# Later second layers, gates rounded by GpSimd and another order of slices, while a fused attention and MLP kernel decodes its weights

## The chip, the cores and the metric

The kernel runs on one core of a Trainium2 chip. The metric is device time in microseconds (us) of one execution; the kernel before takes 677.55 us, the median of three runs (677.43 to 677.74). "Span" is the time from the first to the last instruction of the one profiled execution.

Engines are called as the profile calls them: PE (TensorE, matmuls), PEld (its weight loads), DVE (VectorE), ACT (ScalarE), POOL (GpSimd) and SP (SyncE, which issues the transfers here). Each works through its own list of instructions in order.

## The reference

Attention for 4 sequences of 768 rows and 8 heads of 64, with 8 global and 96 local keys a row and a distance bias, and then an MLP on its output, 3072 rows of 512:

```python
scores = scale * q @ k.T - slope * dist          # masked to local and global keys
x = softmax(scores) @ v                          # 3072 x 512
h = x @ w_in                                     # 512 -> 2048
g = h * clip(h + 3.0, 0.0, 6.0) / 6.0            # the gate
out = g @ w_out                                  # 2048 -> 512, fp32
```

q, k and v are float32. The weights arrive as float64 numbers, of which the core receives the two 32-bit words.

## The kernel before, in words

**Blocks and slices.** The 3072 rows are eight blocks of 384. The hidden width of 2048 is cut into 16 slices of 128. For a slice f of a block b the MLP does a *first layer*, called Fb.f here (`first`, 12 matmuls of L179 into one PSUM bank hp, of which there are two), and a *second layer*, Sb.f (`second`, 9 matmuls of L211, added into three accumulator banks). Every fp32 product is made of three: a high part times both parts of the other, and its low part times the high one. So between the two layers a slice's gate has four steps: ACT adds 3 and clips at 0 (g, L190), DVE clips at 6 and multiplies by h read from PSUM (g, L191), the high part is rounded off (gh: L199 on ACT, or L197 on POOL), and DVE takes the remainder (gl, L204). The tile g has one buffer, so L190 of the next slice waits until gl of this one has read it. gh and gl have three buffers each. In a second layer, of each three matmuls two read gh and one reads gl.

**Decoding.** The weights come in 16 chunks of 1 MB, even ones for first layers and odd ones for second layers: chunk 2k serves the first layers of slices 2k and 2k+1 and chunk 2k+1 their second layers. `decode` turns a chunk's float64 words into a float32 number and splits it in two parts: L384 on ACT and L388 on POOL read the two words, DVE clamps (L417) and shifts (L418), ACT writes signs (L395), DVE adds both words (L427), ACT rounds the high part (L431) and DVE takes the remainder (L424). POOL's result of L388, the tile we, has a single buffer: L388 of the next chunk waits until L427 of this chunk has read it. The raw chunks have two buffers, wz has two.

**Stages.** First, attention of blocks 0 and 1, four pairs of heads each, with the first chunks decoded beside it. Then, as a generator (`halves`), slices of block 0 with some early slices of block 1 between them, while the other chunks are decoded. Then the other slices of block 1, beside which attention of block 2 runs, and from there each block's MLP beside the attention of the next one.

**What sets the order.** The table of `order` says in which sequence slices come. `halves` issues Fb.f, then the second layer of the slice before, and after each piece `work` lets decoding steps out while an estimate of DVE's time is behind one of PE's. On PE, POOL and SP the written order is pinned (`in_order`); on DVE and ACT a scheduler sets it when the program is built. So a POOL instruction that waits holds up all POOL instructions written behind it, and the same goes for a DVE or ACT instruction in the order that the scheduler has given.

Of the kernel before, what the change touches and what calls it, by code (L numbers as in the profile page):

```python
# [26 lines left out]
NF = DF // P  # L27
# [21 lines left out]
LEAD = 6  # L49
WAKE = 9  # L50
BESIDE = 12
LEAST_AHEAD = 4
WORDS = 2
DOWN = 2.0 ** -95

# [7 lines left out]
class Kernel:  # L63
# [377 lines left out]
    def decode_step(self):  # L441
        self.given[1] += next(self.decoding_steps)
        self.decoded += 1
        if self.decoded == 3 * (NF + 1):
            self.decoded_all()

    def decoded_to(self, i):

        while self.decoded < 3 * (i + 1) + (2 if i < NF - 1 else 3):
            self.decode_step()  # L450

    def halves(self, steps, pool=False):


        for block, f, x, acc in steps:
            self.decoded_to(f // 2 * 2)
            g = self.gate(self.first(f, x), block == len(self.blocks) - 1 and f == NF - 1)
            gh = self.high(g, pool) if pool else None
            self.work(2.1, 0.47)
            yield  # L460
            if not pool:
                gh = self.high(g, pool)
            gl = self.rest(g, gh)
            self.work(0, 0.47)
            if self.last is not None:
                self.finish()
                yield
            self.last = (block, f, acc, gh, gl)

    def end(self, steps):  # L470

# [14 lines left out]
        self.second(*late[2], (2,))  # L486

    def finish(self):
        block, f, acc, gh, gl = self.last
        self.decoded_to(f // 2 * 2 + 1)  # L490
        self.second(f, acc, gh, gl)
        if f == NF - 1 and block < len(self.blocks) - 1:
            b, tb = self.blocks[block]
            self.store(b * S + tb * TB, acc)
        self.ended = block, f
        self.work(2.1, 0)
        self.last = None

    def banded(self, flag):

        self.banded_setup()
        start = len(self.nc.cur_bb.bb.instructions)
        self.common(2, 2)
        self.ps_s = self.pool("ps_s", 1, PSUM)
        self.ps_t = self.pool("ps_t", 1, PSUM)
        self.ps_x = self.pool("ps_x", 1, PSUM)
        self.turn, self.more, self.mid, self.score_banks = {}, True, False, 1
        self.wake()
        self.raw, self.z, self.e, self.given, self.decoded = {}, {}, {}, [0.0, 0.0], 0
        self.last, self.op, self.ended = None, None, None  # L510
        self.weights()
        with ExitStack() as early, ExitStack() as words:
            x0 = self.x_tiles(self.pool("x0", 1, ctx=early, side="right"))
            xs = [x0, self.x_tiles(), self.x_tiles()]
            self.decoding(words, WORDS, (2, 1), side="right")
            self.decoding_steps = self.decode()

            def decoded_all():
                words.close()
                self.op = self.pool("op", 2, ctx=early, side="right")  # L520

            self.decoded_all = decoded_all
            self.fetch(0)
            self.given[1] = LEAD
            self.allowed = 3 * NF // 2 + 2
            acc = []
            with ExitStack() as ctx:
                self.room += self.rooms(self.pool("more", 1, ctx=ctx), MORE - ROOMS, ROOMS)
                self.load(2, False)
                self.fetch(1)  # L530
                for n in range(ROOMS):
                    self.load(n, True)
                self.plain_distances(ctx)
                self.attending(ctx, 0, 9, 5)
                pairs = [Pair(self, n, xs[n // NPAIR], True) for n in range(EARLY)]
                acc1 = []
                todo = self.halves(self.order(xs, acc, acc1))
                for n in range(-2, EARLY + 1):
                    if n + 2 < NPAIR:
                        self.distances(n + 2)  # L540
                    if n + 2 == EARLY:
                        self.more = False
                        acc.extend(self.acc_tiles())
                    if n + 2 < EARLY:
                        weigh = []
                        for t in range(NT):
                            weigh.append(pairs[n + 2].scores(t))
                            if n == 0 and t < NT - 1:
                                self.spin(2)
                        if n < 0:  # L550
                            self.spin(5)
                        self.load_next(n + 2, False)
                        self.work(1.440, 0)
                    for t in range(NT):
                        if n + 2 < EARLY:
                            weigh[t]()
                            self.work(0, 0.64)
                            if t == NT - 1 and n == -2:
                                self.load(2, True)
                        if 0 <= n < EARLY:  # L560
                            pairs[n].turn(t)
                            if n == 0 and t < NT - 1:
                                self.spin(3)
                            self.work(0.396, 0)
                        if n + 1 in (0, 1):
                            pairs[n + 1].sum_up(t)
                            pairs[n + 1].normalize(t)
                        if t == 0:
                            if 2 <= n + 1 < EARLY:
                                pairs[n + 1].sum_up()  # L570
                            if not self.more:
                                next(todo)
                        if t == 1:
                            if n > 0:
                                pairs[n - 1].values()
                                self.work(1.350, 0.47)
                            if 2 <= n + 1 < EARLY:
                                for u in range(NT):
                                    pairs[n + 1].normalize(u)
                        if t == 2 and not self.more:  # L580
                            next(todo)
            self.weights()
            self.allowed = 3 * (NF + 1)
            acc1 += [pool.tile([P, BANK], F32, name=name) for pool, name in ((self.ps_s, "sp"), (self.ps_t, "tp"), (self.ps_x, "xp"))]
            while self.ended != (0, NF - 1):
                next(todo)
        self.attending(self.ctx, 2, 4, 2, side="right")
        self.bp = self.pool("bp", 2, side="right")
        self.there = self.pool("there", 2, bass.MemoryType.DRAM)
        self.op = self.pool("op", 2, side="right")  # L590
        self.mid = True
        units = self.beside(xs[2])
        for k, _ in enumerate(todo):
            for unit in units[k] if k < len(units) else ():
                unit()
        self.mid = False
        self.score_banks = 2
        x, ahead = xs[2], None
        for i in range(2, len(self.blocks)):
            units, x_next = [], None  # L600
            if i + 1 < len(self.blocks):
                x_next = self.x_tiles()
                units, ahead = self.attention(i + 1, x_next, ahead)
                if i == 2:
                    units = [[]] + units
            else:
                units = [[]] * 4 + [[lambda: self.doubt(flag)]]
            acc = self.acc_tiles()
            steps = [(i, f, x, acc) for f in range(NF)]
            for k, _ in enumerate(self.halves(steps if x_next else steps[:-3], True)):  # L610
                for unit in units[k] if k < len(units) else ():
                    unit()
            if not x_next:
                self.end(steps[-3:])
            x = x_next
        self.in_order(start)
        return acc

    def order(self, xs, acc, acc1):


        steps, done = [], 0
        for f in range(NF):
            steps.append((0, f, xs[0], acc))
            while done * (NF - LEAST_AHEAD) < (f + 1 - LEAST_AHEAD) * (NF - BESIDE):
                steps.append((1, done, xs[1], acc1))
                done += 1
        return steps + [(1, f, xs[1], acc1) for f in range(done, NF)]
# [406 lines left out]
```

## Time and profile before

| | before |
|---|---|
| median of three runs | 677.55 us (677.43 to 677.74) |
| profiled execution, own time | 679.32 us |
| its span | 677.5 us |
| PE busy | 655.5 us (97%) |
| DVE busy | 406.7 us (60%) |
| ACT busy | 294.3 us (43%) |
| POOL busy | 212.3 us (31%) |
| granted PE clock, mean over the span | 0.989 |

The profiled execution is 1.77 us above the median of the runs. PE is busy nearly everywhere, so time is lost or won only where PE stands still: in attention of the first two blocks and while the weights are decoded, that is, up to about 125 us. Where a row of a view carries a line L..., it is the line of the source; "idle" in brackets is the time for which the engine had waited before the instruction, and what ended it.

### The profile page before, as it was taken

Reading aid. Unit: us, or ns where it says so; the run is one execution under the profiler, and the core shown is the slowest. Engines: PE = TensorE matmul, PEld = TensorE weight load, DVE = VectorE, ACT = ScalarE, POOL = GpSimd, SP = SyncE. Lnnn points to the kernel's source line nnn. Section 1 sums busy time; section 2 is a strip of 40 time slices with the busy share of each in tenths; the row PEclk is TensorE's granted clock in tenths of the full one; section 3 lists DMA queues with packets and bytes.
Section 4 is the critical chain, followed back from the end, with each engine's and each line's share of the span. In section 5 each row is a group of like instructions: output and inputs, shape, how many; then the busy total and the mean of one; then the engine's idle time right before and its main releaser. Section 6 shows DMA issues by size and latency. Waiting matters only on the chain.

```text
span 677.5 us, 11187 instructions
## 1 busy us (share of the span) xinstructions
PE 655.5 (97%) x3923; PEld 582.1 (86%) x3923; DVE 406.7 (60%) x1068; ACT 294.3 (43%) x714; POOL 212.3 (31%) x373
## 2 busy tenths in 40 slices
PE   9878898999998999999999999999999999999997
PEld 7667787898787999999998999899998999999995
DVE  6778899524564776557662677547763677422222
ACT  6988899434553444143332444143331433221111
POOL 5744232001221333325340444404541344302110
PEclk9969899999999999999999999999999999999999
DMA  8645655003575357634554257634455155500001
GB/s 321 185 162 180 247 218 186 1 1 97 153 210 156 98 156 194 171 105 125 153 157 126 91 148 194 172 112 117 125 164 156 62 154 150 139 33 18 1 1 51
DMA packets 67169, 89.56 MB, mean 132 GB/s; under 512 B 10656, under 2 KB 53920, under 8 KB 65056
## 3 DMA queue, kind: packets, MB, share of 16 engines
q1 hardware_dynamic: 66816, 88.49, 43.8%
q8 instruction: 33, 0.54, 0.3%
q14 instruction: 32, 0.26, 0.1%
q10 hardware_dynamic: 288, 0.26, 0.1%
HBM read 65.14 MB, written 23.59 MB: 131 GB/s over the span
## 4 chain that ended last, share of the span: by engine, by line
PE 75%; DVE 9%; DMA 5%; issue 4%; ACT 4%; POOL 2%; SPq 0%; POOLq 0%; DVEq 0%; ACTq 0%
PE hp L179 33%; PE acc L211 31%; PE xp L953 3%; PE sp L866 2%; ACT n L881 2%; DMA load<-pairs 2%; DVE wz L427 2%; PE tp L953 2%; PE tp L866 2%; POOL n L901 1%; DVE n L877 1%; DVE wz L417 1%; DMA wst<-w 1%; DVE g L191 1%; DVE gl L204 1%
## 5 line engine op out<-in xcount | busy, mean ns | idle before, releaser
L190 ACT ACTIVATE g<-hp,small 128x384 f32<-128x384 f32 x127 | 73.6, 580 | 246.0 <-PE hp L179 228.5
L179 PE MATMUL hp<-xh,w1h 128*128 128x384 f32 x512 | 174.6, 341 | 0.0
L179 PE MATMUL hp<-xh,w1l 128*128 128x384 f32 x512 | 172.9, 338 | 0.0
L179 PE MATMUL hp<-xl,w1h 128*128 128x384 f32 x512 | 172.5, 337 | 0.0
L197 POOL TENSOR_SCALAR gh<-g 128x384 fp32r<-128x384 f32 x96 | 51.8, 540 | 296.6 <-DVE g L191 257.5
L211 PE MATMUL acc<-w2h,gl 128*128 128x512 f32 x336 | 133.7, 398 | 5.4 <-DVE gl L204 5.4
L901 POOL TENSOR_SCALAR n<-n,sums 128x232 f32<-128x232 f32 (+1 forms) x186 | 99.0, 548 | 108.6 <-ACT n L881 61.1
L211 PE MATMUL acc<-w2h,gh 128*128 128x512 f32 x336 | 132.4, 394 | 0.4 <-ACT gh L199 0.4
L211 PE MATMUL acc<-w2l,gh 128*128 128x512 f32 x336 | 132.3, 394 | 0.0
L191 DVE SCALAR_TENSOR_TENSOR g<-g,hp 128x384 f32<-128x384 f32 x128 | 69.8, 545 | 89.8 <-ACT g L190 89.4
L881 ACT ACTIVATE n<-n,least 128x232 f32<-128x232 f32 (+1 forms) x192 | 89.2, 466 | 50.5 <-DVE least L877 49.8
L204 DVE TENSOR_TENSOR gl<-g,gh 128x384 fp32r<-128x384 f32 x128 | 78.4, 613 | 52.5 <-POOL gh L197 44.9
L179 PEld LDWEIGHTS hp<-xh,w1h 128*128 128x128 f32 x512 | 96.7, 189 | 6.0 <-issue 2.2
L179 PEld LDWEIGHTS hp<-xl,w1h 128*128 128x128 f32 x512 | 96.7, 189 | 3.7
L179 PEld LDWEIGHTS hp<-xh,w1l 128*128 128x128 f32 x512 | 96.5, 188 | 0.0
L211 PEld LDWEIGHTS acc<-w2h,gl 128*128 128x128 f32 x336 | 63.1, 188 | 23.0 <-DVE gl L204 9.5
L926 DVE STREAM_TRANSPOSE blocks<-n 128x256 f32<-128x256 f32 x132 | 51.5, 425 | 36.3 <-POOL n L901 25.4
L211 PEld LDWEIGHTS acc<-w2h,gh 128*128 128x128 f32 x336 | 63.3, 188 | 10.7 <-ACT gh L199 0.7
L211 PEld LDWEIGHTS acc<-w2l,gh 128*128 128x128 f32 x336 | 63.2, 188 | 10.1
L877 DVE CUSTOM_DVE_ANT_0 n<-sp,d 128x232 f32<-128x232 f32 (+1 forms) x70 | 23.7, 376 | 30.8 <-PE sp L866 30.5
L388 POOL TENSOR_SCALAR we<-wst 128x1024 int32<-128x1024 uint32 x16 | 22.7, 1416 | 46.1 <-DVE wz L427 37.5
L881 ACT ACTIVATION_READ_ACCUMULATOR n<-n,least 128x1 f32 x192 | 36.1, 188 | 0.0
(120 smaller groups left out, 745.6 us busy)
## 6 DMA issues: line engine op xcount, KB each, us to landing
wst<-w SPq DMA_DIRECT2D x16, 1024.0 KB, 4.9
there<-blocks SPq DMA_DIRECT2D x60, 256.0 KB, 2.6
load<-pairs SPq DMA_DIRECT2D x20, 636.0 KB, 5.2
load<-pairs SPq DMA_DIRECT2D x32, 384.0 KB, 4.1
weights<-there SPq DMA_DIRECT2D x48, 192.0 KB, 4.0
weights<-there SPq DMA_DIRECT2D x48, 160.0 KB, 3.2
out<-o SPq DMA_DIRECT2D x23, 256.0 KB, 2.0
load<-pairs SPq DMA_DIRECT2D x11, 444.0 KB, 4.4
```

Of the source, the lines that this page charges most:

```text
L179: self.nc.tensor.matmul(hp, lhsT=self.w1(w, f)[:, kt, :], rhs=a[:, kt, :], start=(n == 0), stop=(n == 3 * NKT - 1))
L190: nc.scalar.activation(out=g, in_=hp, func=AF.Relu, bias=self.three, scale=1.0)
L191: nc.vector.scalar_tensor_tensor(out=g, in0=g, scalar=6.0, in1=hp, op0=ALU.min, op1=ALU.mult)
L197: self.nc.gpsimd.tensor_scalar(out=gh, in0=g, scalar1=1.0, scalar2=0.0, op0=ALU.mult, op1=ALU.add)
L204: self.nc.vector.tensor_tensor(out=gl, in0=g, in1=gh.bitcast(F32), op=ALU.subtract)
L211: self.nc.tensor.matmul(acc[tt], lhsT=a[:, tk], rhs=self.w2(w, f), start=(f == 0 and j == 0), stop=(f == NF - 1 and j == 2))
L866: nc.tensor.matmul(sp[j][:, lo:W], lhsT=q[:, t], rhs=part["kx"][:, c], start=(m == 0), stop=(m == 1))
L877: nc.vector.tensor_tensor_reduce(out=e[:, j, lo:W], in0=sp[j][:, lo:W], in1=d, op0=ALU.add, op1=ALU.min, scale=scale, scalar=3.0e38, accum ...
L881: nc.scalar.activation(out=e[:, j, lo:W], in_=e[:, j, lo:W], func=AF.Exp, bias=self.least[:, i:i + 1], scale=-1.0, accum_out=self.sums[:, ...
L901: nc.gpsimd.tensor_scalar(out=e[:, j, lo:W], in0=e[:, j, lo:W], scalar1=over, scalar2=0.0, op0=ALU.mult, op1=ALU.add)
L926: nc.vector.transpose(out=blocks[:, :, s].rearrange("p b j q -> p j b q"), in_=e[:, :, c:c + P].rearrange("p j (b q) -> p j b q", b=4))
L953: nc.tensor.matmul(xps[j * D:(j + 1) * D, t * P:(t + 1) * P], lhsT=vt[0:K, t, j * D:(j + 1) * D], rhs=self.part(t, j, c, K), start=(c == 0 ...
```

## The change

Three things change; the second reaches a little beyond the decoding.

1. `halves` keeps a list of slices whose second layer is still to come. While chunks remain, Sb.f is issued only when two slices are pending, that is, two first layers later than now; after the last chunk it is one again. And where the chunk of the next first layer isn't yet decoded, a pending second layer is issued ahead of the forced decoding.
2. gh is rounded on POOL (L197), no longer on ACT (L199), for all slices after attention of the first two blocks. Before, POOL did it only from block 2 on; so the slices of block 1 beside attention of block 2 change too.
3. The first four slices of block 1 come between the slices 3 to 7 of block 0, one after each, where they were spread from slice 4 to slice 13. The tables, as F order:

```
before  0.0 0.1 0.2 0.3 0.4 1.0 0.5 0.6 0.7 1.1 0.8 0.9 0.10 1.2 0.11 0.12 0.13 1.3 0.14 0.15 1.4 ...
now     0.0 0.1 0.2 0.3 1.0 0.4 1.1 0.5 1.2 0.6 1.3 0.7 0.8 0.9 0.10 0.11 0.12 0.13 0.14 0.15 1.4 ...
```

From F1.4 on the order of PE is the same as before. No instruction is added or taken away but gh's, which moves from ACT to POOL.

```diff
-LEAST_AHEAD = 4
+LAG = 3
...
+    def ready(self, i):
+        return self.decoded >= 3 * (i + 1) + (2 if i < NF - 1 else 3)
+
     def decoded_to(self, i):
 
-        while self.decoded < 3 * (i + 1) + (2 if i < NF - 1 else 3):
+        while not self.ready(i):
             self.decode_step()
 
-    def halves(self, steps, pool=False):
+    def halves(self, steps):
 
         for block, f, x, acc in steps:
+            while self.last and not self.ready(f // 2 * 2):
+                self.finish()
+                yield
             self.decoded_to(f // 2 * 2)
             g = self.gate(self.first(f, x), block == len(self.blocks) - 1 and f == NF - 1)
+            pool = not self.early
             gh = self.high(g, pool) if pool else None
             self.work(2.1, 0.47)
             yield
...
-            if self.last is not None:
+            while len(self.last) >= (2 if self.decoded < self.all_steps else 1):
                 self.finish()
                 yield
-            self.last = (block, f, acc, gh, gl)
+            self.last.append((block, f, acc, gh, gl))
...
     def finish(self):
-        block, f, acc, gh, gl = self.last
+        block, f, acc, gh, gl = self.last.pop(0)
...
             self.weights()
-            self.allowed = 3 * (NF + 1)
+            self.early = False
+            self.allowed = self.all_steps
...
         for f in range(NF):
             steps.append((0, f, xs[0], acc))
-            while done * (NF - LEAST_AHEAD) < (f + 1 - LEAST_AHEAD) * (NF - BESIDE):
+            if LAG <= f < LAG + NF - BESIDE:
                 steps.append((1, done, xs[1], acc1))
                 done += 1
```

**How the instructions stand on DVE.** One chunk's worth of DVE's list in the middle of the decoding, wz and we being the two words of a chunk, w2l the low parts of decoded weights, g, gh and gl the gate's tiles, and ISA the add of L427. Before:

```order
L204 TENSOR_TENSOR gl<-g,gh 128x384
L427 ISA wz<-wz,we 128x2048
L417 TENSOR_SCALAR wz<-wz 128x1024
L191 SCALAR_TENSOR_TENSOR g<-g,hp 128x384
L418 TENSOR_SCALAR wz<-wz 128x1024
L424 TENSOR_TENSOR w2l_967<-wz,w2h_966 128x1024
L204 TENSOR_TENSOR gl<-g,gh 128x384
```

With the change, the same place:

```order
L191 SCALAR_TENSOR_TENSOR g<-g,hp 128x384
L427 ISA wz<-wz,we 128x2048
L204 TENSOR_TENSOR gl<-g,gh 128x384
L417 TENSOR_SCALAR wz<-wz 128x1024
L418 TENSOR_SCALAR wz<-wz 128x1024
L424 TENSOR_TENSOR w2l_967<-wz,w2h_966 128x1024
L191 SCALAR_TENSOR_TENSOR g<-g,hp 128x384
```

Before, L191 stood between L417 and L418, and gl came three instructions behind it; now only the add L427 stands between L191 and its gl, and gl is followed by L417, L418 and L424 without a gap.

**On POOL**, from the end of the first attention. Before:

```order
L901 TENSOR_SCALAR n<-n,sums 128x232 x6
L388 TENSOR_SCALAR we<-wst 128x1024 x13
L901 TENSOR_SCALAR n<-n,sums 128x128 x2
```

With the change (the two roundings behind the x3 are those of F1.0 and F0.4, and the L388 behind them is that of chunk 6):

```order
L388 TENSOR_SCALAR we<-wst 128x1024 x3
L197 TENSOR_SCALAR gh<-g 128x384 x2
L388 TENSOR_SCALAR we<-wst 128x1024
L197 TENSOR_SCALAR gh<-g 128x384
L388 TENSOR_SCALAR we<-wst 128x1024
L197 TENSOR_SCALAR gh<-g 128x384
L388 TENSOR_SCALAR we<-wst 128x1024
```

POOL had nothing but L388 there; now each L388 stands behind the rounding of a slice. Under the pinned order it can't start until that slice's g is there.

**On DVE, where chunk 6 is decoded**, with the change (the L191 are those of F0.3, F1.0, F0.4 and F1.1, and the L427 is chunk 6's):

```order
L191 SCALAR_TENSOR_TENSOR g<-g,hp 128x384
L417 TENSOR_SCALAR wz<-wz 128x1024
L204 TENSOR_TENSOR gl<-g,gh 128x384
L418 TENSOR_SCALAR wz<-wz 128x1024
L191 SCALAR_TENSOR_TENSOR g<-g,hp 128x384
L204 TENSOR_TENSOR gl<-g,gh 128x384
L191 SCALAR_TENSOR_TENSOR g<-g,hp 128x384
L204 TENSOR_TENSOR gl<-g,gh 128x384
L191 SCALAR_TENSOR_TENSOR g<-g,hp 128x384
L427 ISA wz<-wz,we 128x2048
```

The gates of F1.0, F0.4 and F1.1 now stand ahead of the add of chunk 6. On ACT, too, L395 of chunk 6 stands behind three L190 in a row, those of F1.0, F0.4 and F1.1.

More of the change, by code (lines that the diff above doesn't have):

```diff
@@ L443, in decode_step @@
         self.decoded += 1
-        if self.decoded == 3 * (NF + 1):
+        if self.decoded == self.all_steps:
             self.decoded_all()
+    def ready(self, i):
+        return self.decoded >= 3 * (i + 1) + (2 if i < NF - 1 else 3)
     def decoded_to(self, i):
-        while self.decoded < 3 * (i + 1) + (2 if i < NF - 1 else 3):
+        while not self.ready(i):
             self.decode_step()
-    def halves(self, steps, pool=False):
+    def halves(self, steps):
         for block, f, x, acc in steps:
+            while self.last and not self.ready(f // 2 * 2):
+                self.finish()
+                yield
             self.decoded_to(f // 2 * 2)
             g = self.gate(self.first(f, x), block == len(self.blocks) - 1 and f == NF - 1)
+            pool = not self.early
             gh = self.high(g, pool) if pool else None
@@ L496, in finish @@
         self.work(2.1, 0)
-        self.last = None
     def banded(self, flag):
@@ L509, in banded @@
         self.raw, self.z, self.e, self.given, self.decoded = {}, {}, {}, [0.0, 0.0], 0
-        self.last, self.op, self.ended = None, None, None
+        self.last, self.op, self.ended, self.early, self.all_steps = [], None, None, True, 3 * (NF + 1)
         self.weights()
@@ L609, in banded @@
             steps = [(i, f, x, acc) for f in range(NF)]
-            for k, _ in enumerate(self.halves(steps if x_next else steps[:-3], True)):
+            for k, _ in enumerate(self.halves(steps if x_next else steps[:-3])):
                 for unit in units[k] if k < len(units) else ():
```

## The prediction

> **What bounds the kernel now.** I first looked for the places where PE stands still, in the busy time by stretches of 20 us (columns: stretch and length; busy time and instructions of PE, PEld, DVE, ACT, POOL; granted PE clock; DMA share; GB/s).
>
> ```profile
> 80.00:100.00 20.00, 19.14 (x91) 16.90 (x90) 20.00 (x25) 19.00 (x21) 6.53 (x5) 0.94 0.55 202
> 100.00:120.00 20.00, 18.18 (x88) 15.23 (x87) 20.00 (x25) 19.01 (x22) 6.11 (x5) 1.00 0.48 173
> 140.00:160.00 20.00, 20.00 (x107) 17.91 (x106) 5.32 (x10) 7.69 (x14) 0.00 (x0) 1.00 0.11 40
> ```
>
> From 80 to 120 us DVE is busy for every one of 40 us and ACT for 38, while PE loses 2.7 us. At 140 us PE is full and DVE a quarter busy. So decoding is bound by DVE, and what follows by PE. The period is in DVE's own rows, from one add L427 to the next:
>
> ```profile
> 106.98 1.21 DVE L427 CUSTOM_DVE_ANT_0 wz<-wz,we 128x2048 uint16<-128x2048 uint16 x1
> 108.12 0.68 DVE L417 TENSOR_SCALAR wz<-wz 128x1024 f32<-128x1024 f32 x1
> 108.72 0.54 DVE L191 SCALAR_TENSOR_TENSOR g<-g,hp 128x384 f32<-128x384 f32 x1
> 109.18 1.16 DVE L418 TENSOR_SCALAR wz<-wz 128x1024 int32<-128x1024 int32 x1
> 110.26 1.21 DVE L424 TENSOR_TENSOR w1l<-wz,w1h 128x1024 fp32r<-128x1024 f32 x1
> 111.40 0.54 DVE L204 TENSOR_TENSOR gl<-g,gh 128x384 fp32r<-128x384 f32 x1
> 111.86 1.21 DVE L427 CUSTOM_DVE_ANT_0 wz<-wz,we 128x2048 uint16<-128x2048 uint16 x1
> ```
>
> 111.86 - 106.98 = 4.88 us for a chunk and a slice. From start to start the steps take 1.14 (L427), 0.60 (L417), 0.46 (L191), 1.08 (L418), 1.14 (L424) and 0.46 (gl). PE needs less for a slice: between these two rows, first matmuls of F0.11 and F1.4, it does twelve layers without a gap,
>
> ```profile
> 123.50 0.34 PE L179 MATMUL hp<-xh,w1h 128*128 128x384 f32 x1
> 148.35 0.33 PE L179 MATMUL hp<-xh,w1h 128*128 128x384 f32 x1
> ```
>
> so a layer takes 24.85 / 12 = 2.07 us and a slice 4.14. L418 is 0.48 us longer than L417, its like. The reason is POOL:
>
> ```profile
> 108.28 1.51 POOL L388 TENSOR_SCALAR we<-wst 128x1024 int32<-128x1024 uint32 x1 [3.37 <-DVE wz L427]
> 69.41 1.12 POOL L388 TENSOR_SCALAR we<-wst 128x1024 int32<-128x1024 uint32 x1 [8.23 <-DMA wst<-w]
> 32.93 1.50 POOL L901 TENSOR_SCALAR n<-n,sums 128x232 f32<-128x232 f32 x1
> 32.95 1.24 DVE L427 CUSTOM_DVE_ANT_0 wz<-wz,we 128x2048 uint16<-128x2048 uint16 x1 [1.08 <-ACT we L395]
> 27.55 2.65 POOL L901 TENSOR_SCALAR n<-n,sums 128x232 f32<-128x232 f32 x6 [0.84 <-PE hp L911]
> ```
>
> L388 alone takes 1.12 us, and 1.51 where it starts under L417: it is held until L417 ends at 108.80, runs beside L191, and L418, begun at 109.18, ends 0.55 us after L388 does (109.79). Likewise an L901 of 2.65 / 6 = 0.44 us takes 1.50 under L427 and ends at 34.43, 0.24 after L427. So POOL and some DVE instructions, L427 among them, exclude each other: who comes second waits for the other's end. L191 doesn't take part.
>
> **The change, part by part.** *Counts.* By the order, 17 first and 15 second layers precede the end of decoding before and after, and all DVE work is the same. So it can win only what PE loses there, and can lose by a longer DVE period. I measure both by when F1.4 starts (148.35 now), since PE's order from there is unchanged.
>
> *The period with the change.* DVE: L427, gl, L417, L418, L424, L191. POOL: gh, then L388 of the next chunk. These rows show how the pieces meet:
>
> ```profile
> 591.35 0.51 POOL L197 TENSOR_SCALAR gh<-g 128x384 fp32r<-128x384 f32 x1 [3.66 <-DVE g L191]
> 591.90 0.56 DVE L204 TENSOR_TENSOR gl<-g,gh 128x384 fp32r<-128x384 f32 x1 [0.73 <-POOL gh L197]
> 254.95 0.51 POOL L197 TENSOR_SCALAR gh<-g 128x384 fp32r<-128x384 f32 x1 [4.11 <-DVE g L191]
> 255.42 0.61 POOL L829 TENSOR_SCALAR kx<-load 64x504 fp32r<-64x504 f32 x1
> 255.49 0.94 DVE L204 TENSOR_TENSOR gl<-g,gh 128x384 fp32r<-128x384 f32 x1 [0.70 <-POOL gh L197]
> ```
>
> Left alone, gh takes 0.51 and gl follows 0.04 later. But where POOL has its next instruction ready (kx at 255.42), that one starts 0.04 before gh ends, 0.07 ahead of gl, and gl takes 0.94 for 0.56, ending 0.40 after kx (256.03).
>
> Let L427 start at 0. L191 ended about 0.1 later, so gh finds L427 running and is held to 1.21. It ends about 0.35 after it (an L901 ended 0.24 after; gh is half as wide again), at 1.56. L388 is ready, since we is free at 1.3, and starts at 1.52, ahead of gl; it ends at 1.52 + 1.12 = 2.64. gl ends 0.40 later, 3.04, and the next DVE instruction starts some 0.08 before that, 2.96. Then 0.60 each for L417 and L418 (nothing on POOL disturbs them), 1.14 for L424, 0.46 for L191: 5.76. So the period grows from 4.88 to 5.76 us: DVE is free of L418's 0.48, but waits 0.4 for gh and 1.0 for L388. ACT, relieved of L199, has more room and hides nothing. The bounds: without any exclusion gh would end at 0.8 and L388 hide wholly, so 4.88 - 0.48 = 4.4. If gl were first, and L417, L418 and L424 kept L388 out, it would start beside L191 only, at about 4.4, end at 5.5, and L395 (1.48, below) end at 6.95, when L427 could start. I take 5.76, since 255.42 shows this very race.
>
> *Where that period begins.* Chunk 6 must wait for gates.
>
> ```profile
> 72.36 1.23 DVE L427 CUSTOM_DVE_ANT_0 wz<-wz,we 128x2048 uint16<-128x2048 uint16 x1
> 77.26 1.15 ACT L384 ACTIVATE wz<-wst 128x1024 f32<-128x1024 f32 x1 [0.82 <-DVE w2l L424]
> 77.61 1.22 DVE L427 CUSTOM_DVE_ANT_0 wz<-wz,we 128x2048 uint16<-128x2048 uint16 x1
> 121.65 1.21 DVE L427 CUSTOM_DVE_ANT_0 wz<-wz,we 128x2048 uint16<-128x2048 uint16 x1
> L395 ACT ACTIVATE we<-wst,small 128x1024 f16<-128x1024 int32 x9 | 13.3, 1476 | 0.2
> L190 ACT ACTIVATE g<-hp,small 128x384 f32<-128x384 f32 x10 | 5.8, 576 | 0.7 <-DVE gl L204 0.7
> L431 ACT CAST w1h<-wz 128x1024 fp32r<-128x1024 f32 x5 | 5.3, 1052 | 0.0
> L199 ACT CAST gh<-g 128x384 fp32r<-128x384 f32 x9 | 4.6, 515 | 0.1
> 590.61 0.55 DVE L191 SCALAR_TENSOR_TENSOR g<-g,hp 128x384 f32<-128x384 f32 x1 [2.33 <-ACT g L190]
> 72.20 39.46 SPq L376 DMA_DIRECT2D wst<-w  x9
> wst<-w SPq DMA_DIRECT2D x16, 1024.0 KB, 4.9
> ```
>
> The adds at 72.36 and 77.61 are those of chunks 5 and 6, that at 121.65 the last, chunk 15. Chunk 5 comes as before, because its data does (the 8.23 us wait for it above). Chunk 7 is fetched at 72.20, and is there 4.9 later: L384 for it runs at 77.2 in both. Behind it on ACT, by the new order, stands the rounding of F0.3 (0.5), and on DVE its gl (0.56): 79.5. Now g is free for F1.0: L190 0.58, L191 0.55, 0.19 to POOL, gh 0.51, gl 0.60 with its start, together about 2.45: 82.0. F0.4 the same, but L388 of chunk 6 starts behind its gh and holds gl for 1.0: 85.4. Then L190 of F1.1 and L395 (0.58 + 1.48): the add of chunk 6 starts at about 87.4, 9.8 us later than now. That of chunk 7 follows after 1.21 (L427), 1.05 (L431), L424 with the rest of L388 (1.5) and L191 (0.46), 4.2 in all: 91.6. Eight periods of 5.76 later chunk 15's starts at 137.7, against 121.65.
>
> *PE's end of it.* gl of F0.11 then ends at 137.7 + 1.21 + 0.35 + 0.04 + 0.56 = 139.9. Until then PE can run ahead to S0.10. S0.11 needs that gl for seven of its nine matmuls, 1.6 us: 141.5. F0.13, S0.12, F0.14, S0.13, F0.15 and S0.14 are six layers, 12.4: F1.4 starts at 153.9, 5.5 us later. That the last chunk comes 16 us later but F1.4 only 5.5 is the gain in it: PE has by then done five layers more, 10.4 us.
>
> *The rest.* The list of pending slices keeps PE from waiting on gl (1.89 us once and 0.45 in each period, rows below). That is inside the sum, as the time of F1.4 follows from DVE alone. Moving gh to POOL beside attention of block 2 costs nothing that I can see: PE, full from 140 us on, has two layers (4.1 us) between a first layer and its second, and the gate needs 2.45. If this cover fails, it is some tenths at the four places where POOL's L901 stands ahead of gh: 0 to 1 us, taken as 0.
>
> *PE's clock.* PE would stand still for 5.76 - 4.14 = 1.6 us a period, in two pieces (before S for gl, before F for its bank).
>
> ```profile
> 77.75 0.50 PE L211 MATMUL acc<-w2h,gl 128*128 128x512 f32 x1 [1.89 <-DVE gl L204]
> 79.83 0.52 PE L179 MATMUL hp<-xh,w1h 128*128 128x384 f32 x1
> 82.59 0.34 PE L179 MATMUL hp<-xh,w1h 128*128 128x384 f32 x1
> 107.11 0.50 PE L211 MATMUL sp<-w2h,gl 128*128 128x512 f32 x1 [0.45 <-DVE gl L204]
> ```
>
> After a gap of 1.89 us matmuls of L179 take 0.52 us instead of 0.34, up to about 82.5, and the clock of that stretch is 0.94; gaps of 0.45 leave it at 1.00 (the stretch from 100 to 120). While DVE sets the pace a slower PE costs little, so 0, with up to 2 us at the end of the range. The Trainium skill, "TensorE: Matmul & The Clock Gate", section "Why this matters for your kernels", puts the limit at idle gaps of about 3 us between bursts. The row differs, a shorter gap having been enough, and the row decides; by the page this term would be 0 without an upper bound of 2.
>
> **Sum.** 679.32 (profiled execution: span 677.5 and 1.82 around it) + 5.5 = 684.8, the span 683.0. The median of the runs is 1.77 below the profiled execution, so I predict 677.55 + 5.5 = **683.0 us**.
>
> **Rivals.**
>
> *PE runs ahead and gains (faster).* Place: the same 46 us from chunk 7's to chunk 15's add. Each 0.1 us of the period moves the end by 0.8. Break-even is 5.76 - 5.5 / 8 = 5.07. If gh and L388 slip into gaps of DVE, the period is 4.4 and PE sets the pace: from gl of F0.3 (79.5) on PE needs three layers for S0.3, F1.1 and S1.0, to about 86, and has then 27 layers to F1.4, 55.9 us: 141.9, so 6.5 us faster, 671.1. For it: ACT loses 0.5 us a period, and S no longer waits for gl. Against it: L427 held an L901 for 1.06 us, and gl lost to kx. A middle case, a period of 4.9, gives 91.6 + 39.2 = 130.8, hence 147.0, 1.4 faster: 676.2.
>
> *L388 is starved (slower still).* Period 6.95: 8 x 1.19 = 9.5 more, 692.5. For it: L388 was held behind L417 at 108.28. Against it: POOL was first at 255.42.
>
> *Nothing happens.* DVE's work is the same, so decoding might end as PE needs it: the period would have to be near 5.07 within 0.17. The three queues that I put together by hand could conspire to that, no row speaks for it.
>
> The Trainium skill, "SBUF — State Buffer", section "SBUF: two separate sides", speaks against the change: one port pair is shared by both engines, and a DVE instruction with two SBUF inputs locks it against a GpSimd one that reads SBUF. L427, L424 and gl are such, L191 with PSUM isn't; this agrees with the 1.50 and the 0.94 above, and by that rule the period is 5.76 as well.
>
> **How the numbers follow.** A measurement can't tell less than 0.2%, 1.36 us, from no change. Forecast (period 5.4 to 6.1, ends 680 to 686, with the clock's 2 us 688): 0.58. Starved: 0.07. Middle, period 4.9 to 5.3, 676 to 679.5: 0.20, of which about half is within 0.2% and the rest a bit to each side. PE's pace, 671 to 676: 0.15. So slower 0.67, same 0.11, faster 0.22. The range leaves out the starved case and half of PE's: 673.5 to 688; the forecast's own is 680 to 688.
>
> **What would show it.** Right: DVE's idle time before gl, put down to POOL's gh, some 0.5 us in each period, gl near 1.5 us, L418 near 0.68, L427 to L427 near 5.8, the add of chunk 6 near 87, F1.4 near 154, and beyond that all shifted alike. Wrong: DVE without idle time at 4.9 or less between adds; gh done under L427; or chunk 6 near 80. If PE's stalls beside attention of block 2 grow, the term that I took as 0 fails.

## The result, and the profile after

The changed kernel is slower: 686.99 us, the median of three runs (686.1 to 688.0), which is 1.013 times the kernel before (95% interval 1.0096 to 1.0164), about 9 us more. A fourth run of it took 1634.74 us, far outside what any other run of either kernel took, and is left out. Its profiled execution took 686.99 us with a span of 685.2, against 679.32 and 677.5.

The page of the changed kernel, span and busy time:

```profile
span 685.2 us, 11211 instructions
PE 655.9 (96%) x3923; PEld 582.1 (85%) x3923; DVE 411.2 (60%) x1068; ACT 281.4 (41%) x686; POOL 233.0 (34%) x401
```

PE's work is the same to 0.4 us; the span is 7.7 us longer, so PE stands still longer. Where, shows its busy time by stretches (columns as in the prediction):

```profile
80.00:100.00 20.00, 20.00 (x103) 18.29 (x102) 14.43 (x18) 12.38 (x14) 10.18 (x9) 1.00 0.45 159
100.00:120.00 20.00, 15.28 (x72) 12.41 (x71) 18.64 (x21) 14.06 (x13) 8.52 (x6) 1.00 0.44 157
120.00:140.00 20.00, 13.19 (x63) 11.07 (x63) 18.28 (x22) 13.07 (x13) 9.88 (x7) 0.98 0.31 106
140.00:160.00 20.00, 20.00 (x87) 17.94 (x88) 6.13 (x10) 3.38 (x6) 2.05 (x4) 0.85 0.00 1
```

PE is full from 80 to 100 us and then loses 4.7 and 6.8 us in two stretches in which DVE is busy for more than 18 of 20 us, and it runs at a lower clock from 140 us on. One period of DVE, with what POOL does in it, by the timeline of each:

```profile
102.20 0.55 DVE L191 SCALAR_TENSOR_TENSOR g<-g,hp 128x384 f32<-128x384 f32 x1
102.67 1.22 DVE L427 CUSTOM_DVE_ANT_0 wz<-wz,we 128x2048 uint16<-128x2048 uint16 x1
104.29 0.56 DVE L204 TENSOR_TENSOR gl<-g,gh 128x384 fp32r<-128x384 f32 x1 [0.41 <-POOL gh L197]
104.77 1.60 DVE L417 TENSOR_SCALAR wz<-wz 128x1024 f32<-128x1024 f32 x1
106.41 0.69 DVE L418 TENSOR_SCALAR wz<-wz 128x1024 int32<-128x1024 int32 x1
107.02 1.22 DVE L424 TENSOR_TENSOR w2l<-wz,w2h 128x1024 fp32r<-128x1024 f32 x1
108.15 0.55 DVE L191 SCALAR_TENSOR_TENSOR g<-g,hp 128x384 f32<-128x384 f32 x1
108.61 1.22 DVE L427 CUSTOM_DVE_ANT_0 wz<-wz,we 128x2048 uint16<-128x2048 uint16 x1
```

```profile
102.91 1.35 POOL L197 TENSOR_SCALAR gh<-g 128x384 fp32r<-128x384 f32 x1 [3.03 <-DVE g L191]
104.33 1.49 POOL L388 TENSOR_SCALAR we<-wst 128x1024 int32<-128x1024 uint32 x1
```

From add to add it is 5.94 us where it was 4.88. The rounding gh takes 1.35 us for 0.51: it started at 102.91 under L427 and ended at 104.26, 0.37 us after it, and gl waited 0.41 us for it. L388 started at 104.33, 0.04 after gl, so it had to wait for gl and then had its turn ahead of L417, which takes 1.60 for 0.69. From start to start against the kernel before, the step from L427 to gl is 0.48 us longer (the wait for gh), L417 1.04 longer (L388's turn) and L418 0.47 shorter, as L388 no longer runs into it: together 1.05 of the 1.06 us.

The start of that stretch, as ACT, POOL and DVE show it (chunk 6), and the last add (chunk 15):

```profile
84.11 0.58 ACT L190 ACTIVATE g<-hp,small 128x384 f32<-128x384 f32 x1 [1.94 <-DVE gl L204]
85.02 1.48 ACT L395 ACTIVATE we<-wst,small 128x1024 f16<-128x1024 int32 x1 [0.33 <-POOL we L388]
```

```profile
82.91 0.51 POOL L197 TENSOR_SCALAR gh<-g 128x384 fp32r<-128x384 f32 x1 [2.01 <-DVE g L191]
83.50 1.48 POOL L388 TENSOR_SCALAR we<-wst 128x1024 int32<-128x1024 uint32 x1
```

```profile
83.45 0.56 DVE L204 TENSOR_TENSOR gl<-g,gh 128x384 fp32r<-128x384 f32 x1 [0.70 <-POOL gh L197]
86.52 1.22 DVE L427 CUSTOM_DVE_ANT_0 wz<-wz,we 128x2048 uint16<-128x2048 uint16 x1 [1.25 <-ACT we L395]
138.36 1.22 DVE L427 CUSTOM_DVE_ANT_0 wz<-wz,we 128x2048 uint16<-128x2048 uint16 x1
```

L388 of chunk 6 came only behind the rounding of F0.4, L395 behind L190 of F1.1, and the add at 86.52, 8.9 us later than before. Then PE around the end of decoding: the first matmuls of a first layer amid it, of S0.11, of F0.13 and of F1.4:

```profile
108.75 0.45 PE L179 MATMUL hp<-xh,w1h 128*128 128x384 f32 x1 [1.55 <-DVE g L191]
140.00 0.79 PE L211 MATMUL acc<-w2h,gh 128*128 128x512 f32 x1 [3.06 <-POOL gh L197]
144.01 0.52 PE L179 MATMUL hp<-xh,w1h 128*128 128x384 f32 x1
157.28 0.33 PE L179 MATMUL hp<-xh,w1h 128*128 128x384 f32 x1
```

A first layer waits 1.55 us for DVE's L191, S0.11 3.06 us for gh of F0.11, and after that matmuls run slow: S0.11 takes 4.0 us to the start of F0.13 where a layer takes 2.07, F0.13 2.9. F1.4 starts at 157.28, 8.9 us later than before. From there on 1.2 us comes back, at one place where PE waits for a transfer beside attention of block 2 (1.06 us; it was 2.20). That wait was between 1.00 and 1.94 us in the ten experiments, whatever they changed, so it isn't put down to the change.

### The profile page after: what moved, and what is told of

Its sections match the earlier page's. It is cut to its first block, busy times and chain, and to the rows that moved or that the text cites. A ratio compares the mean times of both kernels' runs of the same rounds, so it can differ in the third digit from the quotient of the medians.

```text
span 685.2 us, 11211 instructions
## 1 busy us (share of the span) xinstructions
PE 655.9 (96%) x3923; PEld 582.1 (85%) x3923; DVE 411.2 (60%) x1068; ACT 281.4 (41%) x686; POOL 233.0 (34%) x401
## 4 chain that ended last, share of the span: by engine, by line
PE 76%; DVE 8%; DMA 5%; ACT 4%; issue 3%; POOL 3%; SPq 0%; POOLq 0%; DVEq 0%; ACTq 0%
PE hp L179 32%; PE acc L211 31%; PE xp L960 3%; DMA wst<-w 3%; DVE wz L417 2%; PE sp L873 2%; ACT n L888 2%; POOL gh L197 2%; PE tp L960 2%; PE tp L873 2%; DMA load<-pairs 1%; DVE g L191 1%; DVE wz L418 1%; DVE gl L204 1%; POOL n L908 1%
## 5 line engine op out<-in xcount | busy, mean ns | idle before, releaser
L197 POOL TENSOR_SCALAR gh<-g 128x384 fp32r<-128x384 f32 x124 | 73.6, 594 | 378.6 <-DVE g L191 339.4
L190 ACT ACTIVATE g<-hp,small 128x384 f32<-128x384 f32 x127 | 73.6, 580 | 254.5 <-PE hp L179 233.1
L191 DVE SCALAR_TENSOR_TENSOR g<-g,hp 128x384 f32<-128x384 f32 x128 | 69.8, 545 | 89.2 <-ACT g L190 88.6
L908 POOL TENSOR_SCALAR n<-n,sums 128x232 f32<-128x232 f32 (+1 forms) x186 | 98.9, 547 | 43.7 <-DVE sums L899 24.6
L211 PEld LDWEIGHTS acc<-w2l,gh 128*128 128x128 f32 x336 | 63.6, 189 | 10.1
L836 POOL TENSOR_SCALAR kx<-load 64x504 fp32r<-64x504 f32 (+1 forms) x40 | 31.3, 781 | 1.6
```

The costliest lines, as they stand in the source:

```text
L190: nc.scalar.activation(out=g, in_=hp, func=AF.Relu, bias=self.three, scale=1.0)
L191: nc.vector.scalar_tensor_tensor(out=g, in0=g, scalar=6.0, in1=hp, op0=ALU.min, op1=ALU.mult)
L197: self.nc.gpsimd.tensor_scalar(out=gh, in0=g, scalar1=1.0, scalar2=0.0, op0=ALU.mult, op1=ALU.add)
L211: self.nc.tensor.matmul(acc[tt], lhsT=a[:, tk], rhs=self.w2(w, f), start=(f == 0 and j == 0), stop=(f == NF - 1 and j == 2))
L836: nc.gpsimd.tensor_scalar(out=part["kx"][own, c], in0=k[own, c], scalar1=1.0, scalar2=0.0, op0=ALU.mult, op1=ALU.add)
L908: nc.gpsimd.tensor_scalar(out=e[:, j, lo:W], in0=e[:, j, lo:W], scalar1=over, scalar2=0.0, op0=ALU.mult, op1=ALU.add)
```

## The experiments

The theory: POOL and most of DVE's decoding instructions exclude each other, so DVE's period is set by what stands beside gh and L388 in DVE's order. The rivals: only the rounding on POOL costs; or the lag, or the order of slices, costs by itself; or chunk 6's late start does. All ten were compared with the kernel before on their own chip, where it took 679.1 to 679.9 us, so ratios are what compares. The table has what the sections below use; "gates ahead" counts the L191 that stand on DVE ahead of chunk 15's add.

| kernel | DVE period | chunk 15's add | gates ahead | F1.4 starts | time over before (95% interval) |
|---|---|---|---|---|---|
| before | 4.88 | 121.65 | 13 | 148.35 | 1 |
| the change | 5.95 | 138.36 | 16 | 157.28 | 1.013 (1.0096 to 1.0164) |
| e1, gh on ACT | 5.34 | 125.31 | 13 | 152.38 | 1.007 (1.0045 to 1.0095) |
| e2, e1 with DVE's old order | 4.88 | 120.19 | 12 | 148.89 | 1.003 (1.0011 to 1.005) |
| e3, slices spread | 5.95 | 141.52 | 16 | 160.40 | 1.0149 (1.0126 to 1.0171) |
| e4, L388 twice | 6.74 | 147.84 | 16 | 164.21 | 1.0235 (1.0204 to 1.0266) |
| e5, lag kept to F0.15 | 5.95 | 138.92 | 16 | 153.60 | 1.0067 (1.0044 to 1.0089) |
| e6, gh on POOL alone | 5.95 | 138.02 | 16 | 154.43 | 1.0069 (1.0042 to 1.0096) |
| e7, slices alone | 4.89 | 119.59 | 13 | 146.24 | 0.9998 (0.9984 to 1.0013) |
| e8, e2 with one gate earlier | 4.89 | 122.38 | 13 | 146.94 | 0.9978 (0.9962 to 0.9994) |
| e9, lag alone | 5.34 | 126.62 | 12 | 157.92 | 1.0151 (1.0125 to 1.0178) |
| e10, e1, POOL after decoding | 5.34 | 125.88 | 13 | 152.95 | 1.0051 (1.003 to 1.0072) |

The start of the decoding moves from one execution to the next (chunk 5's add between 70.3 and 72.4 us, as its data land), so differences of 2 us in the two columns of times mean little by themselves. Counted from chunk 5's add of the same execution, F1.4 follows the measured times: it starts 76.0 us behind it in the kernel before, 85.5 in the change (9.5 more, 8.8 measured), 80.7 in e1 (4.7 more, 4.8 measured) and 86.4 in e9 (10.4 more, 10.3 measured); the widest apart is e3 (12.6 more, 10.1 measured). The period is that of the steady part; single periods of e6 and e9 are longer.

**e1: the rounding back on ACT**

```diff
-            pool = not self.early
+            pool = block >= 2
```

> The change with its second part undone: gh is rounded on ACT as before, lag and slice order stay new. The scheduler then sets DVE's period as L427, L417, gl, L418, L424, L191. Theory (POOL and DVE exclude each other, so what counts is what stands beside L388 on DVE): gl no longer waits for gh and chunk 6 is no longer late (its add near 78), but L388 is held by L417, takes its turn ahead of gl and holds gl for 1.0 us, so the period is 1.14 + 0.60 + 1.4 + 0.60 + 1.14 + 0.46 = 5.35; the add of chunk 15 near 126.5, F1.4 near 153, 681 to 683 us, slower than before even without gh on POOL. Rival (only gh on POOL costs): period 4.9 or less, add of chunk 15 near 121.5, 677.5 or a little faster.

Measured: 1.007, or 4.8 us above before, period 5.34, chunk 15's add 125.31. Its DVE and POOL:

```profile
103.95 1.21 DVE L427 CUSTOM_DVE_ANT_0 wz<-wz,we 128x2048 uint16<-128x2048 uint16 x1
105.09 0.68 DVE L417 TENSOR_SCALAR wz<-wz 128x1024 f32<-128x1024 f32 x1
105.69 1.48 DVE L204 TENSOR_TENSOR gl<-g,gh 128x384 fp32r<-128x384 f32 x1
107.10 0.68 DVE L418 TENSOR_SCALAR wz<-wz 128x1024 int32<-128x1024 int32 x1
```

```profile
105.25 1.52 POOL L388 TENSOR_SCALAR we<-wst 128x1024 int32<-128x1024 uint32 x1 [3.83 <-DVE wz L427]
```

As foreseen: L388 waits for L417, has its turn ahead of gl, and gl takes 1.48 us. So the rounding on POOL isn't the only loss; without it the new order of DVE still costs 0.46 us a period.

**e2: e1 with DVE's order fixed to that of the kernel before.** Each gate's and chunk's DVE instruction is noted as it is written, and chained to the one before it in a fixed order (A is L427, c L417, G L191, s L418, r L424, l gl):

```diff
+DVE_ORDER = "cscsArArcsAGcsrlAcGsrAlrcGsAlcrs" + 9 * "AcGsrl" + "AGrlGlGlGl"
...
+    def pin(self):
+        before = None
+        at = dict.fromkeys(self.noted, 0)
+        for kind in DVE_ORDER:
+            i = self.noted[kind][at[kind]]
+            at[kind] += 1
+            if before is not None:
+                self.tc.add_manual_dep(i, before, mybir.DependencyInfo(
+                    mybir.DependencyClass.NoSync, mybir.DependencyReason.DATA), reason="pin")
+            before = i.name
```

> As e1_round_on_act, but DVE's order while decoding is fixed by hand to that of the kernel before: L427, L417, L191, L418, L424, gl. Theory: L388 runs beside L191 again, L418 takes 1.16, the period is 4.88, the add of chunk 15 near 121.7, and the time 676 to 678, as before. Rival (the lag or the order of slices costs by itself): still 680 to 683, as PE's order is that of the change.

Measured: period 4.88, and 1.003, 2 us above before and 2.8 below e1. I had expected no loss at all. With PE's order of the change the loss of e1 is mostly gone, so most of it was in DVE's order. What is left goes with one gate: in the order that I fixed, L191 of F0.3 comes behind chunk 6's add, so PE waits 2.88 us for it at 78.5 and then runs slow (clock 0.88 from 80 to 100 us), and one gate fewer than before stands ahead of the last add. e8 moves that gate, and so takes both away at once.

**e3: the early slices spread as before**

```diff
-            if LAG <= f < LAG + NF - BESIDE:
+            while done * (NF - LEAST_AHEAD) < (f + 1 - LEAST_AHEAD) * (NF - BESIDE):
```

> The change with its third part undone: the early slices of block 1 are spread as before, lag and gh on POOL stay. DVE's period is that of the change (L427, gl, L417, L418, L424, L191). Theory: period 5.95 as in the change; chunk 7 instead of 6 waits for a chain of three gates behind POOL's queue (add near 88 to 90), chunk 15's add near 136 to 138, 684 to 687 us. Rival (taking four slices at once makes chunk 6 late, and that is the loss): 678 to 680.

Measured: 1.0149, the period 5.95 as in the change. Taking the four slices at once isn't the loss. The time lies a little above what I expected. Chunk 7's add came at 95.58, not at 88 to 90: PE waited 0.9, 1.5 and 1.9 us for gates between 72 and 79 us and ran slow behind that (clock 0.91 from 80 to 100 us), and the first L190 of the chain of three gates waited 2.61 us for PE, so the chain began later than I had counted.

**e4: L388 issued twice**, DVE's order fixed to exactly that of the change

```diff
-        self.nc.gpsimd.tensor_scalar(out=self.e[i], in0=words[:, :, 0].bitcast(U32), ...)
+        for _ in range(1 if self.early else 2):
+            self.nc.gpsimd.tensor_scalar(out=self.e[i], in0=words[:, :, 0].bitcast(U32), ...)
```

> The change with L388 issued twice for each chunk after the first attention (the second writes the same values again), DVE's order fixed by hand to exactly that of the change. POOL stands idle for 3.0 us in each period there, so there is room. Theory (exclusion): the second L388 waits for L417 and then holds L418 for 0.9 to 1.0 us as the first one holds L417; period 6.9, chunk 15's add near 146, the time 693 to 696. Rival (only the latency of gh counts, POOL's other work fits in its idle time): period 5.95 and 686 to 688 as the change.

Measured: 1.0235, 16 us above before. DVE (L206 is gl, L421 the clamp L417, L423 the shift L418), and POOL:

```profile
108.99 0.56 DVE L206 TENSOR_TENSOR gl<-g,gh 128x384 fp32r<-128x384 f32 x1 [0.41 <-POOL gh L199]
109.46 1.62 DVE L421 TENSOR_SCALAR wz<-wz 128x1024 f32<-128x1024 f32 x1
111.12 1.47 DVE L423 TENSOR_SCALAR wz<-wz 128x1024 int32<-128x1024 int32 x1
```

```profile
109.03 3.01 POOL L392 TENSOR_SCALAR we<-wst 128x1024 int32<-128x1024 uint32 x2
```

The two engines take turns: gl, first L388, clamp, second L388, shift. The shift takes 0.78 us longer than in the change, and the period is longer by as much (6.74 for 5.95). DVE pays 0.8 us for 1.1 us more on POOL, although POOL stood idle for 3.0 us a period. As nothing else differs from the change, this is the exclusion shown by itself.

**e5: the lag of two kept to the end of block 0**

```diff
-            while len(self.last) >= (2 if self.decoded < self.all_steps else 1):
+            while len(self.last) >= (2 if self.decoded < self.all_steps or block == 0 and f < NF - 1 else 1):
```

> The change, but a second layer stays two first layers behind up to F0.15, instead of dropping to one as soon as the last chunk is decoded; so F0.13 stands ahead of S0.11. DVE's order is that of the change. Theory (the change's end of decoding adds a loss of its own: PE stands still 3.06 us for gh of F0.11, and its clock falls after it): F0.13 starts at 138 and fills that gap, F1.4 starts near 152.6 instead of 157.3, and the time is 4 to 5 us below that of the change, 682 to 683 where the change has 687. Rival (that gap is hidden later, as PE catches up): as the change, within 1 us.

Measured: 1.0067, 4 us below the change. F0.13 now stands where PE waited for S0.11:

```profile
139.06 0.44 PE L179 MATMUL hp<-xh,w1h 128*128 128x384 f32 x1 [1.55 <-DVE g L191]
```

```profile
153.60 0.33 PE L179 MATMUL hp<-xh,w1h 128*128 128x384 f32 x1
```

Chunk 15's add comes as late as in the change, and F1.4 3.7 us earlier. So the gap before S0.11 and the slow matmuls behind it are a loss of the change of its own.

**e6: the rounding on POOL alone** (first and third part undone)

```diff
-            while self.last and not self.ready(f // 2 * 2):
-                self.finish()
-                yield
...
-            while len(self.last) >= (2 if self.decoded < self.all_steps else 1):
+            while self.last:
...
-            if LAG <= f < LAG + NF - BESIDE:
+            while done * (NF - LEAST_AHEAD) < (f + 1 - LEAST_AHEAD) * (NF - BESIDE):
```

> The second part alone: gh on POOL, with the lag of one and the spread slices of the kernel before. The scheduler gives DVE mostly the change's period (L427, gl, L417, L418, L424, L191). Theory (exclusion, so the second part alone carries the loss): period 5.95, chunk 15's add near 136, 684 to 687. Rival (lag or order carry it): 677 to 679.

Measured: 1.0069, 4.7 us above before, period 5.95 in most places. It loses by itself, though 16 gates ahead of the last add leave less work for PE behind it than the 13 of before (F1.4 comes 16.4 us after the add, where it was 26.7).

**e7: the four slices at once alone** (e1's edit and the first two of e6's)

> The third part alone: the four early slices at once, gh on ACT, lag of one. DVE keeps the order of the kernel before (L427, L417, L191, L418, L424, gl). Theory: period 4.88, the add of chunk 15 near 121.7, as many gates ahead of it as before, so F1.4 near 148.4 and 677 to 678.5, no change to be measured. Rival (taking them at once costs or gains by itself): 2 us or more to either side.

Measured: 0.9998 (0.9984 to 1.0013): no change, and DVE's period as before. One of its rows on PE bears on the clock:

```profile
75.69 0.50 PE L211 MATMUL acc<-w2h,gl 128*128 128x512 f32 x1 [1.88 <-DVE gl L204]
```

Here a gap of 1.88 us stands by itself, and the clock stays at 1.00 in the stretches from 60 to 80 and from 80 to 100 us.

**e8: e2 with one gate earlier**

```diff
-DVE_ORDER = "cscsArArcsAGcsrlAcGsrAlrcGsAlcrs" + 9 * "AcGsrl" + "AGrlGlGlGl"
+DVE_ORDER = "cscsArArcsAGcsrlAcGsrAlrcGsAlcrsGAl" + 9 * "cGsrlA" + "GrlGlGlGl"
```

> The change with gh on ACT and DVE's order fixed by hand as in e2_act_l191_between, but the gate of F0.3 ahead of chunk 6's add instead of behind it, so that one more gate precedes each later chunk. Theory: DVE's period stays 4.88, the stall of PE before F0.4 in e2_act_l191_between (2.88 us, and a slow clock behind it) goes, chunk 15's add near 121, F1.4 near 146, and the time 2 us below the kernel before, 675 to 676.5. Rival (DVE bounds the end whatever PE does earlier): as e2_act_l191_between, 0.3% above the kernel before.

Measured: 0.9978 (0.9962 to 0.9994), about 1.5 us below before: the only one that beats it, by little. The period stays 4.89, PE waits 0.90 us at 77.6 instead of 2.88 at 78.5, and F1.4 starts 24.6 us after chunk 15's add where e2 needed 28.7. The 4.1 us between are one slice on PE, as there is one gate more ahead of the add. e7, with the lag of one, the same 13 gates and the same period, needs 26.7 from the add to F1.4, so with DVE's period kept the lag of two gains about one layer there.

**e9: the lag alone** (e1's edit and the last of e6's)

> The first part alone: the second layer two first layers later while chunks remain, gh on ACT, slices spread as before. The scheduler gives DVE the order of e1_round_on_act (L427, L417, gl, L418, L424, L191), and one gate fewer stands ahead of chunk 15's add than in the kernel before. Theory (the order that the scheduler draws up for DVE under the lag costs, not the lag on PE): gl takes 1.4 to 1.5, period 5.34, chunk 15's add near 126, 681 to 684 where the kernel before has 679.6. Rival (the lag only takes PE's waits for gl away): as the kernel before or up to 2 us faster.

Measured: 1.0151, 10.3 us above before, where I had expected 1.4 to 4.4. The period is 5.34 (one is 7.20) and gl takes 1.46 to 1.50, as foreseen, but I had not priced the gate that is missing ahead of the last add (one slice, 4.1 us: 31.3 us from the add to F1.4, against 27.1 in e1), nor PE's waits of 1.47, 1.68 and 1.61 us between 74 and 81 us, behind which its clock was 0.84 from 80 to 100 us. So taken alone the lag costs more than the whole change.

**e10: e1, with the rounding on POOL from the end of decoding on**

```diff
-            pool = not self.early
+            pool = not self.early and self.decoded >= self.all_steps
```

> As e1_round_on_act (gh on ACT while chunks remain), but gh on POOL from the end of decoding on, beside attention of block 2, as in the change. Theory (that part of the change costs nothing): the decoding as in e1_round_on_act with a period of 5.34, and the time within 1.5 us of e1_round_on_act, 682 to 685; PE's idle time after 160 us below 3 us. Rival (POOL's queue is held there by L901 and delays gl): 2 us or more above e1_round_on_act, with PE waiting on gl after 160 us.

Measured: 1.0051 (1.003 to 1.0072), where e1 has 1.007: the same within the intervals, and from 160 to 235 us PE waits only 1.41 us, for a transfer. The rounding on POOL beside attention of block 2 costs nothing that can be measured.

## Why the prediction was right or wrong

The range and the sign held; the size was six tenths of what came (5.5 us forecast, about 9 measured). The measured 686.99 us lies at the range's far end: without the 2 us that I had added there for the clock, and put at 0 in the sum, it would have ended at 686.

- *DVE bounds the decoding, and POOL and DVE exclude each other.* Right; gh held by L427 (1.35 us) shows it, and so does e4, which differs from the change by the second L388 alone.
- *The period of 5.76 us.* 5.95, and right in each piece but one. I had L388 start ahead of gl, by a race that kx won at 255.42. Here gl won by 0.04 to 0.05 us in every period. So gl took 0.56 and not 1.5, and L417 1.60: L388 then waited for gl, and its hold of 0.92 came a step later. Eight periods make 1.5 us more. Why kx was first there and L388 second here, the runs don't show.
- *Chunk 6's add near 87.4, chunk 7's near 91.6.* 86.52 and 90.75. The 0.9 us is that race again: the hold of 1.0 us on gl of F0.4 didn't happen (gl of F0.3 also ended 0.5 us earlier, which L395, waiting 0.33 us for L388, mostly took back). That by chunk 15 the two misses nearly cancel, 138.36 for 137.7, is luck.
- *PE's end of it, F1.4 at 153.9.* This is the step that was mis-sized: 157.28. From chunk 15's add I counted 16.2 us, and it took 18.9. I had seen that S0.11 must wait for its gate but costed the clock at 0 while DVE sets the pace. Behind the last add PE sets the pace, and just there stood the longest gap, 3.06 us, after which two layers took 6.9 us instead of 4.1. That is the "2 us at the end of the range", and it was 2.8. e5, which fills the gap, has 14.7 us instead of 18.9.
- *PE's clock after waits of 1.6 us a period.* The waits came as one piece of 1.55, not two, and the clock didn't fall: the stretch from 100 to 120 us has 1.00. The row with 1.89 us that I argued from had two matmuls and another wait of 0.42 ahead of it; the 1.88 us of e7, without such a wait just ahead, left the clock at 1.00. So that row didn't show that one gap of this length is enough.
- *The faster rival.* Fell: from chunk 7 on the change never comes to a period under 5.9. But its first condition, that the lag lets PE run on, holds where DVE's period is kept (e8, 1.5 us gained). That I had priced a middle case, with a period of 4.9, at 1.4 is luck: there chunk 7's add was to come at 91.6, and in e8 it came at 83.30.
- *L388 starved.* Fell, in all runs: it always had its turn after the one DVE instruction that was running.
- *Beside attention of block 2, 0.* Right within the intervals (e10).
- *What the period grew by.* I had put it to gh and L388 together. The rows of the change say the same: 0.48 us of waiting for gh, and L388's turn beside L417 instead of L191. But e1 and e2 show that less than that is enough: with gh on ACT the order that the scheduler makes costs 0.46 of the 1.07 us, and this goes when DVE's old order is kept (e2, e8). e1's order isn't that of the change, and gh on POOL in DVE's old order wasn't run, so 0.46 isn't an exact share of the 1.07.
- *How the three parts add up.* I had priced them only together. They don't add: alone the lag costs 10.3 us (e9), the rounding on POOL 4.7 (e6) and the order of slices nothing (e7), and all three together about 9. Beside the lag, taking the slices at once gains 5.5 us (e1 against e9). And beside the lag with spread slices, the rounding on POOL costs nothing more (e3 against e9, 1.0149 and 1.0151), as the last add comes 14.9 us later, but with 16 gates ahead of it instead of 12, and F1.4 then 18.9 us behind it instead of 31.3. The rounding and the slices without the lag weren't run together.

Open is why the scheduler takes L191 away from L388's side on DVE; the runs only show that it does so with the lag alone (e9) and with the rounding alone (e6), and e1 against e2 that the first of these orders costs.

## What to carry to other kernels

Where two engines exclude each other, an engine's idle time is no measure of the room on it: POOL had 3 us idle in each period, and 1.1 us more work there cost 0.8 us of the bound engine. What counts is which instruction of the other engine stands beside the work; before such an engine is given more to do, look at that in the order that the scheduler will really make. And when a producer bounds a stage, count how much of the consumer's work stands ahead of its last piece: a slice more or less there was worth 4.1 us, as much as 0.46 us in each of nine chunks.

## What the runs showed of the hardware that I had not expected

A POOL instruction that waits for DVE goes next even where DVE's following instruction excludes it too and is ready back to back: behind gl (104.29) L388 went ahead of L417, behind L417 (105.09 in e1) ahead of gl, and in e4 the engines alternated twice in a row. And repeated gaps of 1.55 us every 5.95 us left PE's clock at 1.00 (100 to 120 us), as did a gap of 1.88 us in e7, while gaps of 3.06 us (the change) and 2.88 us (e2) lowered it to 0.85 and 0.88 over the stretch behind them, and so did shorter ones close together: 1.47, 1.68 and 1.61 us within 6 us in e9 (0.84).
